# Grouping part-array attention matmuls in the planned order, and three pairs of heads with decay rows from SBUF

## The chip, the cores and the metric

The kernel runs on one core of one Trainium2 chip. The metric is the device time of one execution in microseconds; several executions of a kernel are timed and their median is given.

## The reference

A causal attention with a decay is followed by two feed-forward layers. The attention has 4 batches, 8 heads, 576 positions and 64 elements per head; each layer maps 2304 tokens of 512 elements to 2048 and back. All is float32.

```python
scores = scale * np.matmul(q, k.transpose(0, 1, 3, 2))
cum = np.cumsum(np.maximum(s, 0.0), axis=-1)
bias = -(cum[:, :, :, None] - cum[:, :, None, :])
scores = np.where(causal, -1e9, scores + np.minimum(bias, 0.0))
attn = softmax(scores)                      # along the last axis
x = attn @ v                                # then (tokens, 512)
h = x @ w_in                                # first layer
x = (h * np.clip(h + 3.0, 0.0, 6.0) / 6.0) @ w_out
h = x @ w2_in                               # second layer
out = (h * np.tanh(softplus(h))) @ w2_out
```

## The kernel before

**Stages.** Up to some 413 us the attention and the first layer for the first 1280 tokens run interleaved: the first layer's two matmuls for a slice of 128 of the 2048 inner elements (lines 889 and 929; each product is made of three rounded parts) stand between pieces of attention. Then come the first layer's remaining tokens (lines 1047 and 929) and the second layer in three blocks of columns (lines 1136 and 1220). In these later stages TensorE's matmuls follow each other in one fixed chain.

**Attention.** Heads are taken in pairs, one head on partitions 0 to 63 and one on 64 to 127. The first 256 positions of a batch are done by `small` (sixteen pairs), the rest by `unit` (sixteen pairs). In `small`, the scores of a pair are eight records of matmul (L772; four instructions, each profiled as two passes); each head uses half the rows of the array, so these are part-array matmuls. VectorE adds the decay and takes the maximum (L785), ScalarE takes the exponential (L792), VectorE or ScalarE scale (L812, L810), TensorE transposes (L818, whole array), the copy goes to `v`'s slot, and the product with V (L832) uses half the columns for each head, again part of the array. In `unit` the same steps are L637 (scores; the last tile of 288 columns uses the whole array), L644, L652, L683 (transposes) and L706 (product with V). The result of the first 256 positions goes into `blk`, the operand of the first layer, which can start when two batches' pairs have written the first part of it.

**Decay rows.** The cumulated sums of all heads are made on VectorE in one SBUF tile (`setup_b`), written to DRAM (`cums`), and loaded back for each pair, spread over 128 partitions, into a buffer `cb`; POOL sets the causal part in it (L758). The first pair alone (`fast`) doesn't load: TensorE adds the rows to the scores with a product of a column of the identity and the SBUF tile (L775, 32 rows of the array), and the mask comes from a constant.

**Weights.** They come as 64-bit words, 512 KB for a slice, into `wraw`, and are rebuilt to float32 by a step on ScalarE (L410) and several on VectorE (L420, L437, L451). The sixteen slices of w_in stay in sixteen slots `win`.

**Order.** Nothing in the order is written by hand. `Plan` takes nodes (an engine, a cost, a priority, the buffers they take and free) and makes a list schedule with them: at each moment the node of least priority that is ready, whose engine is free and whose buffers can be had, is put next on its engine. Buffers of a tag have a fixed number of slots (`MAP`). Where TensorE is planned to be idle in the first 70 us, filler matmuls on the identity are put (L352, one for each 0.11 us, at most 24). The instructions stand on each engine in the planned order, and each engine keeps to it. All priorities are worked out from the numbers in `T`. Loads and stores all go through SP's queue, in its order.

Of the kernel before, what the change touches and what calls it, by code (L numbers as in the profile page):

```python
# [10 lines left out]
F32 = mybir.dt.float32  # L11
# [6 lines left out]
NB, NH, S, D = 4, 8, 576, 64  # L18
DM, DFF = 512, 2048
P = 128  # L20
# [20 lines left out]
    "qk": ("att", 2, 7680), "cb": ("att", 2, 9472), "v": ("att", 2, 2560), "pt": ("att", 2, 10240), "nm": ("att", 2, 48),  # L41
    "l": ("att", 2, 48), "qkr": ("att", 1, 3840),
# [9 lines left out]
    xs=2.866, ls=11.367, sm=1.176, sm2=5.378, w0=4.591, w1=9.811, cum=11.658, wo=1.492, blk0=36.145, blk1=12.97,  # L52
    wo2=40.684, wo2r=9.728, win2=7.325, g=23.399, upre=9.483, uhalf=3.818, upost=6.415, uv=-2.503, spre=6.601,
    shalf=-1.839, spost=3.029, pe=5.342, bias=1.691, la=4, la2=2, wp=16.525, p0=-5.836, p1=6.148, p2=6.056, p3=56.106,
    xo0=7.372, lead=9.764, olead=6.509, c0=217.532, cs0=10.808, c1=61.463, cs1=11.269, gap=1.998, slead=4.439,
    p4=77.005, p5=96.709, s0=15.843, s1=21.887, s2=22.005, s3=14.562, s4=46.208, s5=30.366, xo1=5.675, lead1=6.3,
    olead1=5.945, wo3=2.932, gap1=-2.615, ks=0.781,
)
HOP = 0.05
# [23 lines left out]
class Node:  # L83
    __slots__ = ("eng", "cost", "fn", "deps", "prio", "new", "uses", "left", "succ", "ready", "end", "lat", "seq", "slack", "on", "idle", "start", "grant", "one", "bk", "bf", "tried")


class Plan:
# [8 lines left out]
    def add(self, eng, cost, fn, deps=(), prio=0.0, new=(), uses=(), lat=0.0):  # L96
# [9 lines left out]
        n.slack = 0.0  # L106
        n.grant = None
# [49 lines left out]
    def run(self):  # L157
# [22 lines left out]
        ring = 0.0  # L180
        left = len(self.nodes)
        pool.sort(key=lambda n: (n.prio, n.seq))
        while left:
            progress = True
            while progress:
# [3 lines left out]
                for n in pool:  # L189
# [12 lines left out]
                    if not self.can(n):  # L202
                        n.tried = self.ver
                        continue
                    self.take(n)
# [67 lines left out]
def mm_cost(n):  # L273
    return max(0.111, 0.01 + 0.000424 * n)
# [27 lines left out]
def tile_attention_moe_moe(ctx, tc, qk1, qk, v1, s, w_in, w_out, w2_in, w2_out, out):  # L302
# [273 lines left out]
    def unit(b, h, prio, step, dep0, depc, banks):  # L576
# [52 lines left out]
        for i, a, e in ((2, 0, 384), (3, 0, 512), (4, 0, 288), (4, 288, 576)):  # L629
# [9 lines left out]
            prev_s = A("PE", 3 * mm_cost(w) + (0.1 if i == 4 else 0.4), mm, [n_h, n_l, n_m, prev_s], prio, ps if prev_s else [*ps, nm, l], [t])  # L639
# [68 lines left out]
        n_pv = A("PE", 0.25 + 0.00178 * sum(nq - max(0, P * c - q0) for c in range(tb)), pv, n_p + [n_v], post, [po], [pt, vt])  # L708
# [25 lines left out]
    def small(b, h, pair, prio, step, dep0, depc, banks, fi, n_c1, n_id):  # L734
# [4 lines left out]
        raw = Buf("v", [P, 2 * N], F32)  # L739
# [678 lines left out]
```

## Time and profile before

| what | us |
|---|---|
| median of three runs | 947.76 (947.56 to 950.21) |
| the profiled execution | 945.56 |
| its span, first to last instruction | 943.7 |
| TensorE busy | 923.1 (98%) |
| VectorE busy | 721.3 (76%) |
| ScalarE busy | 599.3 (64%) |
| DMA engines, mean share | 71.4% |

The busy time of TensorE counts fillers as well, and a matmul's record lasts longer than its step in a row of matmuls, since they are pipelined. The step from one start to the next is therefore what a matmul costs in a row.

### The profile page before, as it was taken

To read this page: it belongs to the slowest core of one execution; us is meant where nothing else is said; L and a number is where in the kernel's file an instruction comes from. 1 tells how busy PE (TensorE), PEld (TensorE's weight loads), DVE (VectorE), ACT (ScalarE), POOL (GpSimd) and SP (SyncE) were. 2 spreads that over 40 slices of the span, in tenths; PEclk is the share of its full clock that TensorE was granted. 3 is DMA by queue.
4 is the path that set the end of the run, shared out by engine and by line. 5 is a ranking of instruction groups with operands and counts; after the bars stand their busy time and mean duration, and the time that the engine had idled before them with its cause. 6 is when DMAs were issued, how large, how long until landed. Compare 5 with 4: busy or idle time off the path is not lost.

```text
span 943.7 us, 16638 instructions
## 1 busy us (share of the span) xinstructions
PE 923.1 (98%) x5279; PEld 793.5 (84%) x5279; DVE 721.3 (76%) x1750; ACT 599.3 (64%) x1358; POOL 42.8 (5%) x102
## 2 busy tenths in 40 slices
PE   8999999999999999999999999999999999999998
PEld 5666677767777777988888888899999999999998
DVE  6998787977787555379869983987977779677774
ACT  5986776767665566457667544877556765566553
POOL 1111001111000101000000000000000000000000
PEclk8999999999999999999999999999999999999999
DMA  8798977899887876360029996769874498744785
GB/s 284 230 274 291 310 235 246 284 366 366 306 286 255 239 239 192 123 210 24 1 90 323 373 341 222 234 184 313 255 256 125 127 302 256 247 125 124 248 257 185
DMA packets 115350, 220.43 MB, mean 234 GB/s; under 512 B 12896, under 2 KB 51840, under 8 KB 115264
## 3 DMA queue, kind: packets, MB, share of 16 engines
q1 hardware_dynamic: 115264, 219.38, 71.4%
q8 instruction: 42, 0.69, 0.3%
q14 instruction: 44, 0.36, 0.1%
HBM read 176.76 MB, written 42.57 MB: 232 GB/s over the span
## 4 chain that ended last, share of the span: by engine, by line
PE 79%; DMA 10%; DVE 5%; ACT 3%; issue 1%; SPq 0%; POOL 0%; DVEq 0%; ACTq 0%; POOLq 0%
PE b L1220 18%; PE b L929 18%; PE b L1136 17%; PE b L1047 8%; PE b L889 7%; DMA wraw<-in_w_in_dram 4%; PE b L637 3%; PE b L706 3%; PE b L683 3%; DMA cb<-cuml 2%; DMA wraw<-in_w_out_dram 1%; DMA ws<-wtmp 1%; PE b L772 1%; PE b L352 1%; DMA wo<-wos 1%
## 5 line engine op out<-in xcount | busy, mean ns | idle before, releaser
L929 PE MATMUL b<-g,wo 128*128 128x512 f32 (+1 forms) x960 | 225.3, 376 | 0.2 <-DMA wo<-wos 0.2
L929 PEld LDWEIGHTS b<-g,wo 128*128 128x128 f32 x960 | 165.1, 189 | 33.4 <-issue 5.9
L889 PE MATMUL b<-blk,win 128*128 128x512 f32 (+1 forms) x576 | 137.6, 366 | 0.5 <-ACT blk L357 0.5
L1136 PE MATMUL b<-xob 128*128 128x384 f32 x648 | 117.8, 336 | 2.5 <-ACT b L357 1.8
L1136 PEld LDWEIGHTS b<-xob 128*128 128x128 f32 x648 | 112.3, 188 | 5.2 <-ACT b L357 2.7
L889 PEld LDWEIGHTS b<-blk,win 128*128 128x128 f32 x576 | 94.6, 189 | 19.0 <-issue 4.6
L652 ACT ACTIVATE cb<-cb,nm 128x384 f32<-128x384 f32 (+2 forms) x80 | 54.5, 682 | 27.7 <-DVE nm L644 26.3
L1136 PE MATMUL b<-xob,st 128*128 128x384 f32 x360 | 66.4, 336 | 0.9 <-ACT ub L357 0.4
L1136 PEld LDWEIGHTS b<-xob,st 128*128 128x128 f32 x360 | 62.4, 188 | 2.5 <-DVE e L1021 1.1
L458 DVE TENSOR_TENSOR xob<-xob 128x256 fp32r<-128x256 f32 x108 | 45.0, 422 | 22.5 <-ACT xob L357 20.1
L644 DVE CUSTOM_DVE_ANT_0 cb<-b,cb 128x384 f32<-128x384 f32 (+2 forms) x80 | 44.1, 586 | 21.2 <-PE b L637 17.4
L410 ACT ACTIVATE wtmp<-wraw 128x512 f32<-128x512 f32 x58 | 38.4, 666 | 29.4 <-DMA wraw<-in_w_in_dram 13.0
L357 ACT ACTIVATE b<-b 128x384 f32<-128x384 f32 (+1 forms) x64 | 32.1, 502 | 35.4 <-PE b L1136 22.6
L904 DVE TENSOR_TENSOR g<-e,g 128x512 fp32r<-128x512 f32 (+1 forms) x48 | 29.7, 619 | 31.7 <-ACT g L357 31.1
L1220 PE MATMUL b<-wo,xob 128*128 128x384 f32 x276 | 53.1, 334 | 0.0
L357 ACT ACTIVATE g<-win 128x384 fp32r<-128x384 f32 (+1 forms) x54 | 30.3, 568 | 33.3 <-PE b L929 21.5
L357 ACT ACTIVATE xob<-xob 128x256 fp32r<-128x256 f32 (+1 forms) x86 | 39.0, 457 | 17.1 <-DMA xob<-ws 15.7
L357 ACT ACTIVATE pt<-b 128x384 f32<-128x384 f32 (+2 forms) x89 | 42.5, 511 | 9.4 <-PE b L683 9.0
L1220 PEld LDWEIGHTS b<-wo,xob 128*128 128x128 f32 x276 | 48.3, 188 | 0.0
L637 PE MATMUL b<-qk 64*128 64x384 f32 (+2 forms) x288 | 44.7, 366 | 2.5 <-DVE nm L644 1.0
L1047 PE MATMUL b<-xob,wo 128*128 128x512 f32 x192 | 45.8, 392 | 0.3
L437 DVE SCALAR_TENSOR_TENSOR wtmp<-wraw,wtmp 128x512 uint32<-128x512 uint32 x64 | 44.3, 694 | 1.0
(201 smaller groups left out, 1761.2 us busy)
## 6 DMA issues: line engine op xcount, KB each, us to landing
xob<-ws SPq DMA_DIRECT2D x108, 256.0 KB, 3.5
wo<-wos SPq DMA_DIRECT2D x48, 512.0 KB, 5.4
wraw<-in_w_in_dram SPq DMA_DIRECT2D x32, 512.0 KB, 6.1
wraw<-in_w_out_dram SPq DMA_DIRECT2D x32, 512.0 KB, 5.6
st<-ws SPq DMA_DIRECT2D x60, 256.0 KB, 3.3
cb<-cuml SPq DMA_DIRECT2D x16, 896.0 KB, 7.9
xob<-ws SPq DMA_DIRECT2D x108, 128.0 KB, 2.2
ws<-xob SPq DMA_DIRECT2D x52, 256.0 KB, 5.7
```

Source lines behind the costliest of these rows:

```text
L357: nc.scalar.activation(out=out_, in_=in_, func=AF.Copy)
L410: nc.scalar.activation(out=tmp.t, in_=hi, func=AF.Prelu, scale=2.0 ** -112, alpha=-(2.0 ** 32))
L437: nc.vector.scalar_tensor_tensor(out=out_, in0=lo, scalar=29, in1=tu, op0=ALU.logical_shift_right, op1=ALU.bitwise_or)
L458: return a, add("DVE", v1x(n), lambda: nc.vector.tensor_tensor(out=l(), in0=r(l()), in1=r(h()), op=ALU.subtract), [a], prio, (), [buf])
L637: nc.tensor.matmul(out=ps[g].t[:, 0:w], lhsT=t.t[s_, ka, qo:qo + P], rhs=t.t[s_, kb, nk0 + a:nk0 + e], start=k == 0, stop=k == 2)
L644: nc.vector.tensor_tensor_reduce(out=p.t[:, o:o + w], in0=pb.t[:, 0:w], in1=cb.t[:, o:o + w], scale=-0.125, scalar=(3.0e38 if a == 0 else ...
L652: nc.scalar.activation(out=p.t[:, o:o + w], in_=p.t[:, o:o + w], func=AF.Exp, scale=-1.0, bias=nm.t[:, k:k + 1], accum_out=l.t[:, k:k + 1],)
L889: nc.tensor.matmul(out=hps.t[:, 0:N], lhsT=w.t[:, a, P * c:P * (c + 1)], rhs=x.t[:, c, b, 0:N], start=(c == 0 and k == 0), stop=(c == NCC ...
L929: nc.tensor.matmul(out=y[j].t[:, co[j]:co[j] + N], lhsT=wt.t[:, a, P * j:P * (j + 1)], rhs=g.t[:, b, 0:N], start=(f == 0 and k == 0 and no ...
L1047: nc.tensor.matmul(out=bank.t[:, 0:N], lhsT=lhs(a, j), rhs=xo[p].t[:, j, c, :], start=start and j == 0 and k == 0, stop=j == 1 and k == 2, ...
L1136: nc.tensor.matmul(out=bank.t[:, 0:NS], lhsT=w.t[:, a, P * j:P * (j + 1)], rhs=xo[p].t[:, j, b, :], start=start and j == 0 and k == 0, sto ...
L1220: nc.tensor.matmul(out=banks[m].t[:, 0:NS], lhsT=w.t[:, a, P * m:P * (m + 1)], rhs=b.t[:, c, :], start=start and f == 0 and k == 0, stop=f ...
```

## The change

- A node gets a `mode`: 1 for scores that use half the rows, 2 for products with V that use half the columns, 0 else. When TensorE is in a mode and the next node is of another one, the planner takes a ready node of the same mode instead if its priority is within `mw` = 6.281. Out of mode 0 a part-array node is held back for up to `hold` = 2.844 us when no other part-array node is ready and an ordinary one is. The planner's cost of a change of mode is 0.1 us into a mode and 0.207 back; the costs of the nodes themselves lose that part.
- Three pairs are `fast` instead of one. All pairs of the first two batches take their buffers from other tags: q and k in `st` (four slots) for `v`, the decay rows or scores in `win` for `cb` or `g`, V and the transposed rows in `win` for `qk`. The tiles of maxima and sums have four slots instead of two.
- The planner reckons 0.1 us instead of 0.05 for a hop between engines and 1.2 instead of 0.907 for a load's end, and 24 of the numbers in `T` have new values.

```diff
@@ T, the planner's numbers (two of the lines)
-    olead1=5.945, wo3=2.932, gap1=-2.615, ks=0.781,
+    olead1=5.945, wo3=2.932, gap1=-2.615, ks=0.703, mw=6.281, hold=2.844,
 )
-HOP = 0.05
+HOP = 0.1
@@ Plan.run
+                    if mode and n.one == "PE" and n.mode != mode:
+                        m = next((m for m in pool if m.one == "PE" and m.mode and m.ready <= t and m.prio <= n.prio + T["mw"] and m not in went and self.can(m)), None)
+                        if m is not None:
+                            n, best = m, ("PE", m.cost[0], 0.0)
+                    elif not mode and n.mode and now < n.ready + T["hold"] and not any(m.one == "PE" and m.mode and m is not n and m.ready <= t and self.can(m) for m in pool):
+                        m = next((m for m in pool if m.one == "PE" and not m.mode and m.ready <= t and m not in went and self.can(m)), None)
+                        if m is not None:
+                            n, best = m, ("PE", m.cost[0], 0.0)
                     self.take(n)
...
-                    if e == "PE" and now < 20.0:
-                        c *= 1.6
+                    if e == "PE":
+                        if now < 20.0:
+                            c *= 1.6
+                        if n.mode != mode:
+                            c += 0.1 if n.mode else 0.207
+                            mode = n.mode
...
-                        n.end = ring + 0.907
+                        n.end = ring + 1.2
@@ small
-        raw = Buf("v", [P, 2 * N], F32)
-        if fi and pair_no[0] % 2 == 0:
-            cb = Buf("g", [P, 2, 384], F32)
-        else:
-            cb = Buf("cb", [P, 2, 384], F32)
+        raw = Buf("st" if fi else "v", [P, 2 * N], F32)
+        cb = Buf("win" if fi else "cb", [P, 2, 384], F32)
...
-        v = Buf("qk", [P, 4 * D + 768], F32)
+        v = Buf("win" if fi else "qk", [P, 4 * D + 768], F32)
...
-        fast = fi and pair_no[0] <= 1
+        fast = fi and pair_no[0] <= 3
...
-        n_s = A("PE", 2.8 if fast else 0.9, mm, [n_ld, n_m, n_id], prio, pss + [nm, l] + ([cb] if fast else []), [raw] + ([setup_b] if fast else []))
+        n_s = A("PE", (2.8 if pair_no[0] <= 1 else 2.1) if fast else 0.76, mm, [n_ld, n_m, n_id], prio, pss + [nm, l] + ([cb] if fast else []), [raw] + ([setup_b] if fast else []))
+        n_s.mode = 1
```

What the planner makes of it is shown at three places. Line numbers of after stand 13 to 15 higher. First, TensorE behind the first pair of heads. Before, the first pair's scores and decay products (L772, L775) are followed by fillers on the identity:

```order
L772 MATMUL b_174<-v 128x256
L775 MATMUL b_174<-pt,ident 128x256
L772 MATMUL b_175<-v 128x256
L775 MATMUL b_175<-pt,ident 128x256
L352 LDWEIGHTS ident
L352 MATMUL b_254<-ident 128x256
L352 LDWEIGHTS ident
L352 MATMUL b_254<-ident 128x256
```

Now they are followed by the second and the third pair's (L785 and L788 are the same two lines); here is the end of the third, with the transposes (L832) and the products with V (L846) behind it:

```order
L785 MATMUL b_266<-st 128x256
L788 MATMUL b_266<-pt,ident 128x256
L785 MATMUL b_267<-st 128x256
L788 MATMUL b_267<-pt,ident 128x256
L832 MATMUL b_310<-ident,win 128x128 x3
L832 MATMUL b_321<-ident,win 128x128 x3
L832 MATMUL b_332<-ident,win 128x128 x3
L832 MATMUL b_339<-ident,win 128x128 x3
L846 MATMUL b_352<-win 64x256 x2
L846 MATMUL b_352<-win 64x128 x2
L846 MATMUL b_367<-win 64x256 x2
L846 MATMUL b_367<-win 64x128 x2
```

The 24 fillers are gone from there, and the first pair's transposes stand behind three pairs' scores instead of one.

Second, SP's queue in the first microseconds, with what each load waits for (DMAHW is an earlier load's landing). Before, from the third load of w_in on:

```order
L441 DMA wraw_220<-in_w_in_dram 128x512 [waits DMAHW2_49,DMAHW4_49,DVE_49,Activation_49]
L746 DMA v_224<-in_qk1_dram 128x512 [waits DMAHW3_49,PE_49]
L749 DMA cb_229<-cums_69 128x768 [waits DMAHW0_49]
L749 DMA g_233<-cums_69 128x768 [waits DMAHW5_49]
L749 DMA cb_238<-cums_69 128x768 [waits DMAHW6_49]
L441 DMA wraw_242<-in_w_in_dram 128x512 [waits DMAHW7_49,DVE_49,Activation_49]
L441 DMA wraw_297<-in_w_in_dram 128x512 [waits DMAHW2_49,DVE_49,Activation_49]
```

Now, from the sixth pair's load of q and k on to the load behind the fourth of w_in:

```order
L759 DMA st_284<-in_qk1_dram 128x512 [waits DMAHW6_49,PE_49]
L765 DMA win_290<-in_v1_dram 128x2x128 [waits DMAHW7_49]
L762 DMA win_294<-cums_69 128x768 [waits DMAHW0_49]
L765 DMA win_299<-in_v1_dram 128x2x128 [waits DMAHW1_49]
L762 DMA win_302<-cums_69 128x768 [waits DMAHW2_49]
L765 DMA win_307<-in_v1_dram 128x2x128 [waits DMAHW3_49]
L762 DMA win_314<-cums_69 128x768 [waits DMAHW4_49]
L759 DMA st_319<-in_qk1_dram 128x512 [waits DMAHW5_49,PE_49]
L455 DMA wraw_329<-in_w_in_dram 128x512 [waits DMAHW6_49,DVE_49,Activation_49]
L759 DMA st_411<-in_qk1_dram 128x512 [waits DMAHW7_49,PE_49]
```

The fourth load of w_in has moved behind two loads of q and k that wait for TensorE to have used the slot of an earlier pair.

Third, TensorE in the middle, around a product with V (L706 before, L721 now) of a `unit` pair. Before, it stands alone between transposes or scores and the first layer's matmuls:

```order
L637 MATMUL b_2787<-qk 128x288 x3
L637 MATMUL b_2793<-qk 128x288 x3
L889 MATMUL b_2766<-blk,win 128x512 x3
L706 MATMUL b_2803<-pt,v 64x320 x6
L706 MATMUL b_2803<-pt,v 64x192 x2
L706 MATMUL b_2803<-pt,v 64x64 x2
L929 MATMUL b_2822<-g,wo 128x512 x3
```

Now two pairs' products stand together:

```order
L944 MATMUL b_2549<-g,wo 128x512 x3
L721 MATMUL b_2775<-pt,v 64x320 x6
L721 MATMUL b_2775<-pt,v 64x192 x2
L721 MATMUL b_2775<-pt,v 64x64 x2
L721 MATMUL b_2792<-pt,v 64x320 x6
L721 MATMUL b_2792<-pt,v 64x192 x2
L721 MATMUL b_2792<-pt,v 64x64 x2
L944 MATMUL b_2563<-g,wo 128x512 x3
```

Over the whole program the blocks of part-array matmuls are 66 instead of 74, the fillers 83 instead of 113, and the instructions of every other kind on TensorE as many as before but for eight more decay products.

## Rows read from the trace of the kernel before

**Rows 1.** The page, busy time (us), share and instructions of each engine:

```profile
PE 923.1 (98%) x5279; PEld 793.5 (84%) x5279; DVE 721.3 (76%) x1750; ACT 599.3 (64%) x1358; POOL 42.8 (5%) x102
```

**Rows 2.** Stretches: length, then busy us of PE, PEld, DVE, ACT, POOL; clock; DMA share; GB/s:

```profile
26.40:54.00 27.60, 25.42 (x198) 17.79 (x195) 25.22 (x95) 24.43 (x83) 5.42 (x10) 1.00 0.83 255
54.00:70.00 16.00, 15.97 (x92) 11.22 (x90) 14.63 (x46) 14.55 (x39) 1.24 (x3) 1.00 0.91 263
70.00:413.00 343.00, 335.37 (x2077) 259.34 (x2074) 239.05 (x616) 218.85 (x502) 31.77 (x74) 1.00 0.81 268
```

**Rows 3.** Stretches of the start, for the granted clock (third number from the end):

```profile
5.70:9.00 3.30, 3.30 (x17) 2.00 (x15) 2.26 (x5) 0.66 (x1) 0.00 (x0) 1.00 0.88 274
9.20:11.40 2.20, 2.20 (x4) 0.87 (x4) 1.51 (x4) 1.18 (x2) 0.00 (x0) 0.50 0.83 291
12.40:15.80 3.40, 3.40 (x17) 2.34 (x18) 3.13 (x11) 3.27 (x13) 0.00 (x0) 0.50 0.90 264
```

**Rows 4.** Timeline of TensorE, 0 to 72 us: start, length (us), instruction, count:

```profile
6.18 0.48 PE L772 MATMUL b<-v 64*128 64x128 f32 x2
6.59 0.48 PE L775 MATMUL b<-pt,ident 32*128 32x128 f32 x2
...
7.83 0.70 PE L772 MATMUL b<-v 64*128 64x256 f32 x2
...
9.08 1.22 PE L772 MATMUL b<-v 64*128 64x256 f32 x2
10.23 1.22 PE L775 MATMUL b<-pt,ident 32*128 32x256 f32 x2
12.36 4.51 PE L352 MATMUL b<-ident 128*128 128x256 bf16 x24 [0.91 <-DVE nm L785]
16.71 0.82 PE L818 MATMUL b<-ident,g 128*128 128x128 f32 x6
...
18.30 1.58 PE L772 MATMUL b<-v 64*128 64x128 f32 x16
...
37.83 1.38 PE L352 MATMUL b<-ident 128*128 128x256 bf16 x11
39.04 0.83 PE L818 MATMUL b<-ident,cb 128*128 128x128 f32 x6
...
53.35 0.82 PE L818 MATMUL b<-ident,cb 128*128 128x128 f32 x6
```

**Rows 5.** Chain that ended last, 0 to 72 us: start, length without the overlap:

```profile
35.80 0.86 PE b L772 x8
...
37.09 0.80 PE b L832 x8
...
39.20 0.66 PE b L818 x6
```

**Rows 6.** Timeline of TensorE around one part-array block of the middle:

```profile
124.64 0.39 PE L929 MATMUL b<-g,wo 128*128 128x512 f32 x1
124.96 0.93 PE L772 MATMUL b<-v 64*128 64x128 f32 x8
125.81 2.35 PE L889 MATMUL b<-blk,win 128*128 128x512 f32 x9
128.00 0.82 PE L683 MATMUL b<-ident,cb 128*128 128x128 f32 x6
```

**Rows 7.** Chain that ended last, whole span: a long run of like matmuls:

```profile
496.62 87.07 PE b L929 x384
```

**Rows 8.** Timeline of POOL, 0 to 60 us: the first mask on loaded decay rows:

```profile
17.28 0.77 POOL L758 TENSOR_SCALAR_AFFINE_SELECT cb<-cb 128x256 f32<-128x256 f32 x2 [15.35 <-DMA cb<-cums]
```

**Rows 9.** Waits of TensorE, 70 to 413 us: total us, times, longest:

```profile
PE b L706 <- DMA v<-in_v_dram: 2.1, 1, 2.1
PE b L683 <- ACT cb L672: 1.3, 1, 1.3
```

**Rows 10.** Timeline of SP's queue, 0 to 72 us: fourth and fifth load of w_in:

```profile
12.68 3.87 SPq L441 DMA_DIRECT2D wraw<-in_w_in_dram  x2
```

More of the change, by code (lines that the diff above doesn't have):

```diff
@@ L40 @@
     "g": ("main", 2, 4096), "e0": ("main", 2, 2048), "st": ("main", 4, 2048), "wo": ("main", 3, 4096), "G1": ("main", 1, 3072),
-    "qk": ("att", 2, 7680), "cb": ("att", 2, 9472), "v": ("att", 2, 2560), "pt": ("att", 2, 10240), "nm": ("att", 2, 48),
-    "l": ("att", 2, 48), "qkr": ("att", 1, 3840),
+    "qk": ("att", 2, 7680), "cb": ("att", 2, 9472), "v": ("att", 2, 2560), "pt": ("att", 2, 10240), "nm": ("att", 4, 48),
+    "l": ("att", 4, 48), "qkr": ("att", 1, 3840),
     "xob": ("late", 1, 57344), "ub": ("late", 1, 6144),
@@ L83 @@
 class Node:
-    __slots__ = ("eng", "cost", "fn", "deps", "prio", "new", "uses", "left", "succ", "ready", "end", "lat", "seq", "slack", "on", "idle", "start", "grant", "one", "bk", "bf", "tried")
+    __slots__ = ("eng", "cost", "fn", "deps", "prio", "new", "uses", "left", "succ", "ready", "end", "lat", "seq", "slack", "on", "idle", "start", "grant", "one", "bk", "bf", "tried", "mode")
 class Plan:
@@ L106, in add @@
         n.slack = 0.0
+        n.mode = 0
         n.grant = None
@@ L180, in run @@
         ring = 0.0
+        mode = 0
         left = len(self.nodes)
@@ L638, in mm @@
                                          start=k == 0, stop=k == 2)
-            prev_s = A("PE", 3 * mm_cost(w) + (0.1 if i == 4 else 0.4), mm, [n_h, n_l, n_m, prev_s], prio, ps if prev_s else [*ps, nm, l], [t])
+            prev_s = A("PE", 3 * mm_cost(w) + (0.0 if i == 4 else 0.12), mm, [n_h, n_l, n_m, prev_s], prio, ps if prev_s else [*ps, nm, l], [t])
+            prev_s.mode = 0 if i == 4 else 1
             for g in range(len(ps)):
@@ L707, in pv @@
                                      start=c == 0, stop=c == tb - 1)
-        n_pv = A("PE", 0.25 + 0.00178 * sum(nq - max(0, P * c - q0) for c in range(tb)), pv, n_p + [n_v], post, [po], [pt, vt])
+        n_pv = A("PE", -0.06 + 0.00178 * sum(nq - max(0, P * c - q0) for c in range(tb)), pv, n_p + [n_v], post, [po], [pt, vt])
+        n_pv.mode = 2
         t0 = token(b, q0)
@@ L833, in pv @@
                                          rhs=v.t[:, 4 * D + 384 * g + 2 * a:4 * D + 384 * g + 2 * a + N - a], start=c == 0 and lhs is None, stop=c == 1)
-        n_pv = A("PE", 1.95 if fz else 0.9, pv, n_p + [n_v], post, [po, pn] if fz else [po], [v])
+        n_pv = A("PE", 1.75 if fz else 0.7, pv, n_p + [n_v], post, [po, pn] if fz else [po], [v])
+        n_pv.mode = 2
         pt_nodes.append(n_pv)
@@ L842, in small @@
         if fz:
-            held = Buf("st", [P, 512], F32)
+            held = Buf("e0", [P, 512], F32)
             src = lambda: held.t[:, 0:N]
```

12 lines of the change are left out of this document (6 added, 6 removed).

## Prediction

> **What bounds the kernel now.** I read the page first: TensorE is busy for 98% of the span [rows 1]. So time is won or lost where TensorE idles, runs filler matmuls, runs at the low clock, or is slowed between two kinds of work. The table of stretches shows where that is [rows 2]. From 70 to 413 us, in which attention and the first feed-forward layer are interleaved, TensorE is idle 7.6 of 343 us. Before 54 us things stand otherwise: from 26.4 to 54, VectorE and ScalarE are busy 25.2 and 24.4 of 27.6 us, and TensorE's share holds many fillers (L352): 89 of the program's 113 stand behind the first pair of heads. From 54 us on TensorE has hardly a gap. The start-up is thus a stretch with three near-full engines, and every microsecond that it gains or loses is passed on to the end, since nothing behind 54 us can absorb it.
>
> In the start the timeline of TensorE and the granted clock belong together [rows 3, 4]. The first pair A takes its decay rows from SBUF: each score product (L772, 64 rows) is followed by a decay product (L775, 32 rows) into the same bank. The clock granted is 1.00 (2.4 GHz) from 5.7 to 9 us and 0.50 (1.2 GHz) from 9.2 to 11.4 us, although TensorE has run without a pause; it comes back only after 3.5 us of full-array fillers, at some 15.9 us. The second pair's scores start at 18.30, since POOL had its decay rows only at 17.28 [rows 4, 8].
>
> **The change, part by part. (1) Two more pairs, B and C, take decay rows from SBUF.** Removed: two broadcast loads of 384 KB, two POOL masks, the wait to 17.28 and the 24 fillers from 12.36 to 16.7. Added: eight score products more slowly run and eight decay products. Prices: at the high clock 0.41 us for each 128-column product (6.18 to 6.59) and 0.63 for each of 256 columns (two from 7.83 to 9.08), so a pair is 4 x 0.41 + 4 x 0.63 = 4.15 us. At the low clock 256 columns take 1.15 (9.08 to 10.23) [rows 4]. 128 columns were not seen there; the difference of 0.22 between the two sizes doubles with a halved clock, which gives 0.72, and a pair 7.5 us. A pair with loaded rows is 0.86 [rows 5]. So the two pairs add 6.6 us of TensorE time at the high clock and 13.3 at the low one. I take the low one: the order has nothing but such products from A to the end of C, and it is these under which the clock fell. A ends at 11.45 as before, B at 18.95, C at 26.45.
>
> A page of the Trainium skill speaks of this too: "TensorE: Matmul & The Clock Gate", in its part on packing small matmuls, says that matmuls in distinct row groups run concurrently. By it the products of a pair's second head (rows 64 to 127) would run beside decay products (rows 0 to 31), and a pair would be a quarter shorter, the sum some 2 us less at the high clock. The row disagrees: products of 128 columns follow one another at 0.41 us whichever head they belong to [rows 4].
>
> From 26.45 I add up what the new order has on TensorE until the ninth pair's transposes are done, which before was 53.35 + 0.66 = 54.0 [rows 4, 5]: 9 transposes of 0.66, 8 products with V (L832) of 0.80, 7 scores of 0.86, 9 matmuls of the first layer at 0.227 [rows 7] and 52 fillers at 0.11 (eleven from 37.83 to 39.04): 5.9 + 6.4 + 6.0 + 2.0 + 5.7 = 26.0 us. Before, the same list from 16.7 on (with 8 scores, 21 first-layer matmuls and 65 fillers) makes 31.2 us and took 37.3, so 6.1 were waits and switches. I take 3.5 for after, since VectorE and ScalarE have been waiting for B and C and stand ready: 55.95. At that point 12 first-layer matmuls are still to do that had been done (2.7), one score is done that had not (0.86), and 7 fillers come later (0.8): 1.95 + 2.7 - 0.9 + 0.8 = **4.6 us lost** (4.55); with waits between 2 and 6.1, 3.1 to 7.2; at the high clock 2.1 gained. VectorE now waits for B's scores before it scales A's rows, which costs nothing, since A's transposes stand behind C's scores on TensorE in any case.
>
> **(2) First pairs in unused weight slots** (tags win and st for cb, g, qk, v) cost no instruction. They let loads go out early, but st has four slots: the fifth pair's load of q and k waits for A's scores, the sixth for B's, the seventh for C's, and SP is one queue. Behind the seventh stands the fourth load of w_in, so at 26.5 instead of 12.7 to 16.5 us [rows 10]. On SP and POOL the broadcasts and masks of two later pairs (tag cb) also stand ahead of the fourth pair's, whose scores are not due before some 30 us, 12 us after A to C's loads are through. I cost all this at nothing, since TensorE needs that weight only after some 56 us; without this cover it is the second rival below.
>
> **(3) Grouping.** The order has 66 blocks of part-array matmuls for 74. Behind the ninth pair 58 entries into a mode become 52, and 57 exits to the full array 48. A block's price is read at 124.64 us: the block starts 0.32 us after a second-layer matmul that is followed by the next at 0.227 (87.07 us for 384) [rows 6, 7]. From there to 128.00 are 3.36 us: one matmul and nine of the first layer make 2.27, so the eight score products cost 1.09. Eight that follow eight of their own kind add only 1.58 - 0.93 = 0.65 [rows 4, 6]. So a lone block costs 0.44 too much, about half of it at each end: 6 x 0.2 + 9 x 0.2 = **3.0 us gained**; bounds 1.9 (an entry at 0.32 - 0.227 = 0.09, an exit at the 0.15 by which the nine matmuls behind the block took longer) and 4.0 (nine whole blocks at 0.44).
>
> **(4) New priorities and latencies** in the planner (a hop 0.1 for 0.05 us, an SP load 1.2 for 0.907) reorder all engines. That no row shows. Of the 7.6 idle us from 70 to 413 the largest are single waits, 2.1 us for a V load and 1.3 us for a scaling on ScalarE [rows 2, 9]; a plan that reckons with later landings should meet fewer. Bounds: all of it gone, or 3 more. I take **2.0 gained**. Behind 413 us each matmul chain keeps its order: nothing.
>
> The sum is 4.6 - 3.0 - 2.0 = -0.4 us. The profiled execution took 945.56 (its span 943.7, 1.9 around it), which makes 945.2; the median of the runs shown, 947.76, stands 2.2 above it, so **947.4 us**. Its own range is about 942.5 to 952. A measurement of this kernel can tell about 0.3%, 2.8 us, from no change.
>
> **The rivals.** First: the clock is back, or stays, during B and C. For it: TensorE never pauses there, and at the low clock products of 256 columns fill it more evenly. Against it: the fall at 9.1 us in the midst of the same products [rows 3]. Then C ends 6.7 us earlier (13.3 - 6.6): 940.7. The Trainium skill's page "TensorE: Matmul & The Clock Gate", part on the clock gate, is on this side: it ties the high clock to a busy TensorE and the low one to an idle one. This case's rows speak against it, as the clock fell with no idle time before it.
>
> Second, slower: the held SP queue. With the seventh pair's load of q and k waiting for C's scores, weight loads four and five go out 10 us late or more, and those behind them with them. The DMA engines are 83% busy from 26.4 to 54, 91% to 70 and 81% to 413 [rows 2]. Some four loads of 512 KB, at 263 GB/s 2.0 us each, are 8 us of transfer that has to be fitted in again; if only 3 us of it find room before their readers come, TensorE waits 5: 952.4. It decides if TensorE idles for weights (blk,win or g,wo products) between 56 and 120 us.
>
> Third: the new order removes nearly all idle time of the middle, 7 us in place of 2, with the pairs at the low clock: 942.4. For it is that the big waits are few and single; against it, that a fixed order makes new ones where durations differ from the plan's, and the plan is 9 us out as soon as C ends (it gives the three pairs 11.2 us, the rows above 20).
>
> That the change would not group at all is excluded by the order itself.
>
> **How the numbers follow.** Forecast 0.41, high clock 0.26, held queue 0.22, middle emptied 0.11. Faster by over 0.3%: nearly all of the high clock and of the emptied middle, 0.36; slower: the held queue, 0.22; the rest, 0.42. The range goes from 940 (high clock, 940.7, with a little room) to 953 (held queue), which leaves out the farther halves of those two, under 0.2.
>
> **What will show it.** The third pair's last decay product ends at 26.5 us with the clock at 0.50 from 9 us on (low), or near 20 (high). The ninth pair's transposes end near 56 us. The fourth w_in load goes out right behind the third pair's scores. TensorE's idle time from 70 to 413 is 5 to 6 us, and its part-array blocks cost no more each than now. I am wrong on step 1 if C ends before 23 us, on step 2 if weights are waited for, on step 4 if the idle time of the middle rises.

## The result, and the profile after

| what | before | after |
|---|---|---|
| median, us | 947.76 (946.94 to 950.21, 7 runs) | 941.09 (936.26 to 942.68, 7 runs) |
| ratio of the medians | | 0.9918, 95% interval 0.9900 to 0.9936 |
| the profiled execution, us | 945.56 | 939.11 |
| its span, us | 943.7 | 937.3 |

The changed kernel is 0.8% faster, more than the 0.3% that can be told from no change. The forecast of little change, 947.4, was wrong; the time lies inside the range. By the number alone it is nearest to the first rival (940.7), but that is chance: what the trace shows is the third (942.4), as the clock stayed low under the three pairs and the middle lost its idle time. The page of after, the busy time of the engines:

```profile
PE 926.8 (99%) x5265; PEld 798.0 (85%) x5265; DVE 717.0 (76%) x1740; ACT 594.4 (63%) x1368; POOL 40.8 (4%) x98
```

The busy time of TensorE is larger than before [rows 1] in a shorter span, since slower products count as busy. The stretches show more (columns as in [rows 2]):

```profile
26.40:57.00 30.60, 29.56 (x234) 20.81 (x235) 24.57 (x113) 26.65 (x95) 2.60 (x6) 0.93 0.37 126
...
70.00:413.00 343.00, 341.06 (x2134) 267.32 (x2133) 250.81 (x647) 228.09 (x520) 30.88 (x72) 1.00 0.84 278
...
577.00:937.00 360.00, 354.77 (x2028) 351.11 (x2027) 272.48 (x606) 222.91 (x514) 0.00 (x0) 1.00 0.70 220
```

From 70 to 413 us TensorE's idle time is 343 - 341.06 = 1.9 us, where it was 7.6 [rows 2]. Its waits from 57 to 406 us (total us, times, longest) are three, and neither of those in [rows 9] is among them:

```profile
PE b L651 <- DVE nm L659: 1.1, 1, 1.1
PE b L698 <- ACT pt L371: 0.4, 1, 0.4
PE b L904 <- DVE e L916: 0.2, 1, 0.2
```

The DMA engines' share behind 26.4 us fell from 0.83 to 0.37. The start, first by its clock (stretches again), then on TensorE's timeline:

```profile
6.74:10.10 3.36, 3.36 (x14) 1.96 (x14) 1.08 (x3) 0.09 (x1) 0.00 (x0) 1.00 0.98 354
10.20:30.60 20.40, 20.40 (x57) 12.03 (x58) 10.07 (x41) 10.03 (x34) 5.29 (x12) 0.50 0.88 297
30.70:34.00 3.30, 2.92 (x28) 1.98 (x25) 2.50 (x12) 0.81 (x3) 0.00 (x0) 1.00 0.00 0
```

```profile
11.33 0.79 PE L785 MATMUL b<-st 64*128 64x128 f32 x2
12.05 0.79 PE L788 MATMUL b<-pt,ident 32*128 32x128 f32 x2
...
25.11 1.22 PE L788 MATMUL b<-pt,ident 32*128 32x256 f32 x2
26.26 2.82 PE L832 MATMUL b<-ident,win 128*128 128x128 f32 x12
...
56.35 0.94 PE L832 MATMUL b<-ident,cb 128*128 128x128 f32 x6
57.12 3.98 PE L904 MATMUL b<-blk,win 128*128 128x512 f32 x15
```

The third pair ends at 26.26 us, at the low clock from 10.2 us on. Two landmarks behind it, on the same timeline: the first matmul of the first layer's rest (L1047, after L1062) and of the second layer (L1136, after L1151), of before and then of after:

```profile
416.19 1.55 PE L1047 MATMUL b<-xob,win 128*128 128x512 f32 x6
...
583.53 1.22 PE L1136 MATMUL b<-xob 128*128 128x384 f32 x6
```

```profile
412.47 1.54 PE L1062 MATMUL b<-xob,win 128*128 128x512 f32 x6
...
579.55 1.22 PE L1151 MATMUL b<-xob 128*128 128x384 f32 x6
```

So after is 3.0 us late at the ninth pair's transposes (56.35 + 0.66 = 57.0, against 54.0), 3.7 early at the first layer's rest, 4.0 early at the second layer, and 6.4 early at the end. The gain was made in the interleaved middle, and some 2.4 us more in the second layer.

### The profile page after: what moved, and what is told of

The parts are those of the page before. It is cut to its first block, busy times and chain, and to the rows that moved or that the text cites. A ratio compares the mean times of both kernels' runs of the same rounds, so it can differ in the third digit from the quotient of the medians.

```text
span 937.3 us, 16531 instructions
## 1 busy us (share of the span) xinstructions
PE 926.8 (99%) x5265; PEld 798.0 (85%) x5265; DVE 717.0 (76%) x1740; ACT 594.4 (63%) x1368; POOL 40.8 (4%) x98
## 4 chain that ended last, share of the span: by engine, by line
PE 90%; DVE 4%; DMA 3%; ACT 2%; issue 1%; SPq 0%; POOL 0%; DVEq 0%; POOLq 0%; ACTq 0%
PE b L944 20%; PE b L1235 19%; PE b L1151 18%; PE b L904 10%; PE b L1062 8%; PE b L651 4%; PE b L721 3%; PE b L698 3%; PE b L785 2%; DMA wraw<-in_w_in_dram 1%; DMA wraw<-in_w_out_dram 1%; PE b L788 1%; PE b L366 1%; PE b L832 1%; PE b L846 1%
## 5 line engine op out<-in xcount | busy, mean ns | idle before, releaser
L944 PE MATMUL b<-g,wo 128*128 128x512 f32 (+1 forms) x960 | 223.2, 375 | 0.0
L944 PEld LDWEIGHTS b<-g,wo 128*128 128x128 f32 x960 | 165.2, 189 | 31.4 <-issue 4.7
L904 PE MATMUL b<-blk,win 128*128 128x512 f32 (+1 forms) x576 | 134.0, 365 | 0.2 <-DVE e L916 0.2
L1151 PE MATMUL b<-xob 128*128 128x384 f32 x660 | 121.7, 336 | 1.4 <-ACT b L371 1.2
L1151 PEld LDWEIGHTS b<-xob 128*128 128x128 f32 x660 | 114.7, 188 | 3.5 <-ACT b L371 1.8
L1151 PE MATMUL b<-xob,st 128*128 128x384 f32 x348 | 66.0, 335 | 0.6 <-ACT b L371 0.6
L371 ACT ACTIVATE g<-win 128x384 fp32r<-128x384 f32 (+1 forms) x57 | 32.3, 571 | 47.4 <-PE b L944 32.2
L1151 PEld LDWEIGHTS b<-xob,st 128*128 128x128 f32 x348 | 60.6, 188 | 1.4 <-ACT b L371 0.9
L371 ACT ACTIVATE xob<-xob 128x256 fp32r<-128x256 f32 (+1 forms) x107 | 45.8, 432 | 15.7 <-DMA xob<-ws 8.0
L424 ACT ACTIVATE wtmp<-wraw 128x512 f32<-128x512 f32 x58 | 38.9, 670 | 25.9 <-DMA wraw<-in_w_in_dram 13.8
L651 PE MATMUL b<-qk 128*128 128x288 f32 (+2 forms) x288 | 45.0, 363 | 1.1 <-DVE nm L659 1.1
L1062 PE MATMUL b<-xob,wo 128*128 128x512 f32 x192 | 45.6, 390 | 0.6 <-DVE xob L1020 0.6
L371 ACT ACTIVATE pt<-b 128x384 f32<-128x384 f32 (+2 forms) x85 | 40.6, 512 | 8.3 <-PE b L698 8.0
```

Of the source, the lines that this page charges most:

```text
L371: nc.scalar.activation(out=out_, in_=in_, func=AF.Copy)
L424: nc.scalar.activation(out=tmp.t, in_=hi, func=AF.Prelu, scale=2.0 ** -112, alpha=-(2.0 ** 32))
L651: nc.tensor.matmul(out=ps[g].t[:, 0:w], lhsT=t.t[s_, ka, qo:qo + P], rhs=t.t[s_, kb, nk0 + a:nk0 + e], start=k == 0, stop=k == 2)
L904: nc.tensor.matmul(out=hps.t[:, 0:N], lhsT=w.t[:, a, P * c:P * (c + 1)], rhs=x.t[:, c, b, 0:N], start=(c == 0 and k == 0), stop=(c == NCC ...
L944: nc.tensor.matmul(out=y[j].t[:, co[j]:co[j] + N], lhsT=wt.t[:, a, P * j:P * (j + 1)], rhs=g.t[:, b, 0:N], start=(f == 0 and k == 0 and no ...
L1062: nc.tensor.matmul(out=bank.t[:, 0:N], lhsT=lhs(a, j), rhs=xo[p].t[:, j, c, :], start=start and j == 0 and k == 0, stop=j == 1 and k == 2, ...
```

## The experiments

Two kinds were run. Some undo a part and let the planner make its order anew; the others hold the order of the changed kernel, instruction for instruction, and alter what one step costs.

**One fast pair instead of three, planned anew.**

```diff
-        fast = fi and pair_no[0] <= 3
+        fast = fi and pair_no[0] <= 1
```

> After with one pair of heads taking its decay rows from SBUF instead of three; the other first pairs keep the weight slots as buffers, grouping and new numbers stay, and the planner orders anew. Theory (the start-up of after is 4.8 us behind that of before at the ninth pair's transposes, and is passed on to the end): about 936 us, the ninth pair's transposes near 53 us instead of 57. Rival (the slow start costs nothing in the end, since later engines would have waited anyway): 940 to 942, with the gain at 55 us given back by 400.

944.71 us (943.43 to 947.07; ratio to before 0.9972, 0.9959 to 0.9985). The ninth pair's transposes are done 2.8 us earlier than in after: the matmul behind them starts at 54.36 for 57.12 us. At the first matmul of the first layer's rest nothing of that is left. It starts at 409.78 us, 2.7 earlier than in after, but 24 of the products of L944 that after has done by then, 0.12 us each, are still to come, 2.9 us. So it was lost in the middle and, next, at the handover from the interleaved middle to the first layer's rest. Two stretches, then the waits of TensorE in the second (total us, times, longest):

```profile
70.00:406.00 336.00, 331.41 (x2046) 255.39 (x2047) 241.28 (x632) 217.46 (x493) 32.05 (x72) 1.00 0.82 270
406.00:440.00 34.00, 30.34 (x165) 25.31 (x165) 32.94 (x58) 22.02 (x43) 0.00 (x0) 1.00 0.32 114
```

```profile
PE b L1062 <- ACT wo L371: 2.3, 2, 1.8
PE b L1062 <- DVE wo L518: 1.4, 2, 0.8
```

TensorE idles 4.6 us from 70 to 406, where after idles 1.9 (336 - 334.06), and 3.7 us at the handover, where after idles 0.59. The next run, with three pairs, has the same wait at the handover; so it goes with the new order and not with the number of pairs, and this run doesn't price the pairs.

**No grouping, planned anew.** The two preferences of the planner are never taken; its reckoned cost of a change of mode stays.

```diff
-                    if mode and n.one == "PE" and n.mode != mode:
+                    if False:
...
-                    elif not mode and n.mode and now < n.ready + T["hold"] and ...
+                    elif False and not mode and n.mode and now < n.ready + T["hold"] and ...
```

> After without the planner's two preferences for part-array blocks (the cost of a change of mode stays in its reckoning, so do the new numbers and the three pairs); 75 entries and 69 exits instead of 66 and 59. Theory (grouping is worth the changes it saves, nine entries and ten exits at about 0.2 us each): 3 to 4 us slower than after, 944 to 945, TensorE's idle time from 70 to 406 still about 2 us. Rival (grouping is also what removed the waits of the middle): 948 or more, idle time back at 6 to 8 us.

951.08 us (946.79 to 954.79; 1.0032, 1.0016 to 1.0049). From 70 to 406 us TensorE idles only 2.6 us, but at the handover stands the same wait (L1062 for ScalarE, 2.3 us in two waits):

```profile
406.00:440.00 34.00, 31.39 (x181) 26.71 (x180) 31.38 (x54) 20.44 (x42) 0.00 (x0) 0.95 0.43 147
```

The mean clock of that stretch is 0.95. By its time the run is the rival's, but the idle time of the middle did not come back, though the rival expected it to. So this run doesn't price the grouping alone either.

**Old numbers and latencies, planned anew**: T's values, HOP 0.05 and 0.907 as before, the rest as in after.

```diff
-HOP = 0.1
+HOP = 0.05
...
-                        n.end = ring + 1.2
+                        n.end = ring + 0.907
```

> After with the 22 old numbers, the hop at 0.05 and a load's end at 0.907; three pairs and grouping stay (64 entries, 60 exits). Theory (the new numbers removed some 5.7 us of waits of TensorE from 70 to 406 and 2.4 in the second layer): 947 to 950, idle time of the middle back at 6 to 8 us. Rival (grouping did it): 940 to 943.

959.27 us (957.15 to 963.87; 1.0135, 1.0105 to 1.0165), worse than either theory had it: 9.1 us idle from 70 to 406.

**Before, with the new numbers and latencies.**

```diff
-HOP = 0.05
+HOP = 0.1
```

> Before with the new numbers and latencies alone; one pair with rows from SBUF, no grouping, old buffers. Theory (the numbers alone remove the waits, and no slow start is paid): 939 to 941. Rival (the numbers are fitted to the rest of the change and do nothing alone): 946 to 950.

949.02 us (946.75 to 954.34; 1.0024, 1.0002 to 1.0047). Without the rest the new numbers bring nothing.

**Neighbours of the order.** The runs planned anew raised the question of what any other order costs. Three kernels move nearly all numbers of the planner by up to 1% at random; two are neighbours of after, one of before.

```diff
-    xs=2.866, ls=10.945, sm=1.176, sm2=5.326, w0=4.591, w1=9.811, cum=11.527, wo=1.492, blk0=29.215, blk1=14.81,
+    xs=2.845, ls=11.021, sm=1.182, sm2=5.3, w0=4.591, w1=9.801, cum=11.562, wo=1.501, blk0=28.978, blk1=14.67,
```

> The changed kernel with all of the planner's numbers but the two of the grouping moved by up to 1% at random, so that nothing that the change does is undone and the order is merely another of its neighbours (66 entries into part-array modes and 62 exits, for 66 and 59; 117 fillers for 83). It asks how much of the gain hangs on this one fitted order. Theory (the gain is that this order, as executed, has few waits; a neighbour has them again): 945 to 951, with idle time of TensorE from 70 to 406 us back above 3 us or a wait of some us at the handover to the first layer's rest behind 406 us. Rival (the gain comes from what the edits do, and neighbours have it too): 940 to 943.

> The changed kernel nudged by another draw of up to 1% (69 entries into part-array modes, 64 exits, 94 fillers). The first draw gave 961.5, of which 6.8 us were one wait at 420 us for VectorE and 3.0 one at 70 us. Theory (a neighbour has a few single large waits, at other places each time): 946 to 962, with one or two waits of TensorE above 1.5 us between 60 and 430 us. Rival (the first draw was an unlucky one): 940 to 944.

> The kernel before with all of its planner's numbers moved by up to 1% at random, with the same draw as in the nudged changed kernel. It asks if before was as closely fitted. Theory (each kernel's numbers were fitted until its order had few waits, so a neighbour of either is slower by several us): 952 to 968. Rival (before was an ordinary order and the changed kernel a lucky one): 944 to 950, as often below before's median as above it.

They took 961.53 (957.1 to 963.53), 959.17 (955.62 to 961.91) and 955.98 us (953.56 to 958.56): 20.4 and 18.1 us above after, 8.5 above before. Waits of TensorE in the first:

```profile
PE b L944 <- DVE g L919: 6.8, 1, 6.8
PE b L366 <- DVE nm L659: 2.8, 1, 2.8
```

and in the second:

```profile
PE b L944 <- DVE g L919: 8.8, 1, 8.8
PE b L366 <- DVE nm L659: 3.1, 1, 3.1
```

Two large waits stand in each. They were expected at other places each time, but stand at the same ones: the larger ends at the handover, at 427.7 and 426.6 us, the smaller in the middle, at 73.2 and 74.8. A 1% change of numbers that undoes nothing costs as much as undoing the numbers wholly, and more than undoing the grouping. None of the runs planned anew can therefore be put down to its edit. Such a wait also has a tail; stretches of the first neighbour (the clock is the third number from the end):

```profile
420.00:424.00 4.00, 0.88 (x5) 0.49 (x3) 4.00 (x5) 3.61 (x5) 0.00 (x0) 0.99 0.76 228
424.00:428.00 4.00, 0.29 (x1) 0.29 (x2) 3.99 (x5) 0.25 (x1) 0.00 (x0) 0.50 0.13 48
428.00:432.00 4.00, 4.00 (x25) 4.00 (x25) 1.92 (x6) 0.95 (x3) 0.00 (x0) 0.66 0.00 0
```

After 6.8 us without work the clock is at 0.50 (1.2 GHz), and TensorE's first 4 us behind the wait run at 0.66 in the mean.

**The order held: the start without decay products of B and C.**

```diff
+        decay = fi and pair_no[0] <= 1
...
-                                     start=True, stop=not fast)
-                    if fast:
+                                     start=True, stop=not decay)
+                    if decay:
```

> The changed kernel in its own order, instruction for instruction, but the second and the third pair leave out their decay products, so the decay is missing for the first 256 positions of four heads. It asks whether time won in the first 26 us arrives at the end when the order is held. In the changed kernel the third pair ends at 26.3 us (each pair 7.5 us, clock 0.50), the ninth pair's transposes at 57.0, and the median was 941.1. Theory (the start-up costs what the sum said, and is passed on whole): the eight score products of a pair take 0.86 us, so the third pair ends by some 13 us, limited by its load; VectorE and ScalarE, which were starved to 26 us, then set the pace to 57, and the ninth pair's transposes end 6 to 10 us earlier; the end comes as much earlier, 931 to 935. Rival A (the order was fitted to the late start: loads that were early enough are now late): the ninth pair's transposes end earlier by as much, but at the first matmul of the first layer's rest (412.5 us in the changed kernel) only half of it is left, 936 to 939. Rival B (VectorE and the masks set the pace to 57 us in any case): 940 or more.

933.07 us (930.87 to 934.04), 8.0 below after. The third pair is done by 13.8 us, but then TensorE waits. Its timeline:

```profile
11.63 2.15 PE L786 MATMUL b<-st 64*128 64x128 f32 x8 [1.18 <-issue]
15.24 1.51 PE L833 MATMUL b<-ident,win 128*128 128x128 f32 x6 [1.46 <-ACT win L807]
17.58 1.54 PE L833 MATMUL b<-ident,win 128*128 128x128 f32 x6 [0.82 <-ACT win L825]
19.05 2.51 PE L847 MATMUL b<-win 128*64 128x256 f32 x16
```

The products with V start at 19.05 us, 10.0 earlier than in after (29.01), and the first layer's rest at 402.95, 9.5 earlier. Of the 10.0, 1.2 belong to the execution and not to the edit, as the first pair began at 5.37 for 6.60 us. Time won in the start passes nearly whole through the middle; rivals A and B fall. The span is 8.2 us shorter (929.1): 1.3 are lost in the second layer.

**The order held: scores first, then decay products (SSDD for SDSD).**

```diff
-                    if fast:
-                        nc.tensor.matmul(
+                for g in range(2 if fast else 0):
+                    nc.tensor.matmul(
```

> The changed kernel in its own order, but inside each of the three first pairs the score products of both heads stand first and their two decay products behind them, for either half of the columns: SSDD where it was SDSD. It asks whether it is the alternation of 64-row and 32-row products that makes a product cost 0.41 us at the high clock and 0.72 at the low one (two heads' scores in a row are some 0.11 us each elsewhere in the program), and that goes with the fall of the clock at 10.2 us. Theory (the alternation costs most of it): a pair falls from 7.5 to some 5 us, the third pair ends at 17 to 21 us, the end comes 2 to 5 us earlier, 936 to 939. Rival (the price lies in the 32-row products themselves, or in the clock, whatever the order): the third pair ends at 25 to 27 us and the time is 940 to 942.

932.50 us (931.34 to 933.35; ratio to before 0.9845, 0.9819 to 0.9871): better than the theory had it. TensorE's timeline, the first pair and the end of the third, then a stretch for the clock:

```profile
6.60 0.49 PE L785 MATMUL b<-st 64*128 64x128 f32 x4
7.02 0.71 PE L788 MATMUL b<-pt,ident 32*128 32x128 f32 x4
...
9.34 0.49 PE L785 MATMUL b<-st 64*128 64x128 f32 x4
...
18.89 2.82 PE L832 MATMUL b<-ident,win 128*128 128x128 f32 x12
```

```profile
10.20:22.00 11.80, 11.80 (x41) 7.75 (x42) 9.21 (x40) 7.98 (x30) 2.39 (x6) 0.50 1.03 369
```

At the high clock a pair takes 2.74 us (6.60 to 9.34) for 4.15, and the third ends at 18.89 us for 26.26. Both executions begin the first pair at 6.60 us, so these 7.4 us are the edit's; the span is 7.8 shorter (929.6). Two heads' 128-column scores take 0.42 us together (6.60 to 7.02), as much as a single product did in the alternation [rows 4]. The clock still falls to 0.50.

The Trainium skill's page "TensorE: Matmul & The Clock Gate", in its part on packing small matmuls, says that matmuls in distinct row groups run concurrently. The trace agrees for the two heads' scores, rows 0 to 63 and 64 to 127, when they stand together.

**The order held: decay products on all 128 rows.** The tile of sums is cleared once.

```diff
+        nc.vector.memset(setup_b.t[:, 0:384], 0.0)
...
-  lhsT=ident[0:NB * NH, row + g:row + g + 1].to_broadcast([NB * NH, P]),
-  rhs=rows()[3][:, COFF[i]:COFF[i] + CW[i]],
+  lhsT=ident[:, row + g:row + g + 1].to_broadcast([P, P]),
+  rhs=setup_b.t[:, COFF[i]:COFF[i] + CW[i]],
```

> The changed kernel in its own order, but the decay products of the three first pairs use all 128 rows of the array: the tile of sums is cleared once on all partitions, by one more VectorE step of 384 columns in the first microseconds, and the product takes the identity's whole column. It asks whether the clock falls at 10.2 us because these products leave most rows of the array unused. Theory: with 128 rows in half of the products the clock stays at 1.00 in 10.2 to 26 us, or comes back early, the third pair ends near 20 us as in the rival of the prediction, and the end comes 4 to 6 us earlier, 935 to 937. Rival (the clock falls in any case): third pair at 26 us, 940 to 942; if a change between 64 and 128 rows costs more than one between 64 and 32, up to 944.

932.47 us (930.43 to 933.73; ratio 0.9841, 0.9816 to 0.9867). The clock, and the end of the third pair on the timeline:

```profile
5.70:18.00 12.30, 12.30 (x49) 7.16 (x49) 10.02 (x39) 6.49 (x22) 0.00 (x0) 1.00 1.04 377
```

```profile
17.53 0.70 PE L789 MATMUL b<-pt,ident 128*128 128x256 f32 x2
18.06 1.62 PE L833 MATMUL b<-ident,win 128*128 128x128 f32 x12
```

The clock holds at 1.00 through the three pairs. That is no chance of this execution: the mean granted clock of the whole span is 1.000 in all six executions of this kernel, and 0.989 to 0.991 in the seven of after. Products in alternation cost 0.41 and 0.63 us as before, so the alternation's price is the same for 32 and 128 rows, and only the clock differs. The third pair ends 8.2 us earlier, 1.0 of it because the first began at 5.64 for 6.60 us, and the span is 8.7 shorter (928.6).

**Both together.** 

> The changed kernel in its own order with the two edits of before put together: inside the three first pairs both heads' scores and then both decay products, and decay products on all 128 rows. Each edit alone gave 932.5. At the high clock a pair in this order took 2.74 us (the first pair of that run, 6.60 to 9.34), so with the clock held three pairs end 8.2 us behind 5.64, at 13.9 us, where the pairs of either edit alone ended at 18 to 19. Theory (it was the time of the three pairs that cost, and the rest follows): the clock stays at 1.00 and the end comes up to 4 us earlier, 928.5 to 930. Rival (below 18 us VectorE and ScalarE set the pace, as in the run without decay products, whose scores were done at 13.8 and whose transposes still waited for ScalarE until 15.2 and 17.6): no more than 1.5 us earlier, 931 to 933, with idle time of TensorE behind the third pair and perhaps the low clock after it.

930.90 us (929.25 to 933.13; ratio 0.9817, 0.9791 to 0.9842), the fastest kernel here, though its interval overlaps those of either edit alone. TensorE's timeline, the second pair's end, the third's begin, and the second transposes, then a stretch for the clock:

```profile
9.98 1.13 PE L789 MATMUL b<-pt,ident 128*128 128x256 f32 x4
12.24 0.99 PE L786 MATMUL b<-st 64*128 64x128 f32 x4 [1.13 <-issue]
...
18.19 0.92 PE L833 MATMUL b<-ident,win 128*128 128x128 f32 x6 [0.53 <-ACT win L825]
```

```profile
11.10:18.00 6.90, 5.39 (x23) 3.72 (x22) 6.76 (x31) 5.63 (x21) 0.00 (x0) 0.75 1.05 373
```

The second pair ends 1.13 us before the third can start, and the products with V start at 19.05 as without decay products. The time lies between the theory and the rival; the timeline is the rival's: below some 18 us the pairs are no longer what bounds the start. The clock did not hold here: behind the wait of 1.13 us it fell to 0.50 at 14.6 us, in the third pair, for all that the decay products use 128 rows, and was back at 18.0.

**The order held: six blocks taken apart again**, on the kernel with full-row decay products. Where two blocks of one mode stand together behind 70 us, the second is moved behind the next whole-array node.

```diff
+            if b.start < 70.0 or not a.mode or a.mode != b.mode or c.mode:
+                continue
...
+            order.insert(j, order.pop(i))
```

> The kernel with full-row decay products (932.5 us) in its own order but for TensorE's in six places behind 70 us, where two blocks of the same part-array mode stand together: there the second block is moved behind the next whole-array node. So six more blocks are entered and left, which is about what the grouping of the change saved (66 entries for 74), and nothing else moves by more than that node's length. It prices the grouping with the order held, which no replanned kernel could. Theory (a lone block costs 0.44 us too much, as the prediction read it, with 0.24 as its lower bound): the stretch from the ninth pair's transposes (47.0 us) to the first matmul of the first layer's rest (403.4) grows by 1.4 to 2.6 us and the time is 934 to 935. Rival (much of a block's price is hidden, or lies elsewhere): the stretch grows by less than 0.8 us and the time is 932 to 933. If moving the six blocks makes new waits of TensorE, these are read from the trace and taken out.

934.63 us (933.8 to 937.52) for 932.47. Side by side with the kernel without the moves, TensorE's sequence is later from just before each move to the second matmul behind it, where the delay settles, by 0.35, 0.34, 0.34, 0.39, 0.39 and 0.33 us, 2.1 in all. So a block costs 0.36 us, and the stretch grows as the theory had it. The profiled execution, the slowest of the four, is some 4.8 us later still at the first layer's rest, which is not the moves' own price. Most of that, 3.5 us, comes in one place behind the third move, where scores now wait for VectorE. TensorE's timeline, and a stretch behind it for the clock:

```profile
176.26 2.33 PE L922 MATMUL b<-blk,win 128*128 128x512 f32 x9
179.99 1.44 PE L669 MATMUL b<-qk 64*128 64x512 f32 x6 [1.40 <-DVE nm L677]
```

```profile
180.00:184.00 4.00, 4.00 (x14) 2.77 (x15) 2.85 (x8) 2.89 (x9) 1.15 (x3) 0.72 0.94 325
```

The wait is 1.40 us; most of the rest comes with the clock, 0.72 in the 4 us behind it.

The Trainium skill's page "TensorEngine Tiling (Array Packing)" says under "Key Properties" that a change of tiling mode drains the engine. The trace agrees in so far as a change costs time, 0.36 us here for a way in and out; the drain itself it doesn't show.

**Old late numbers.** Five of the planner's numbers as before (`ls` stands in another line); TensorE's order differs from the second layer on alone.

```diff
-    xo0=7.036, lead=9.764, olead=8.187, ..., gap=0.466, slead=4.334,
+    xo0=7.372, lead=9.764, olead=6.509, ..., gap=1.998, slead=4.439,
```

> The changed kernel with five of the planner's numbers (ls, olead, xo0, gap, slead) put back to their values of before. The order is the same instruction for instruction up to the first matmuls of the second layer and differs behind that alone. It asks what of the gain is made in the second layer, which the prediction took to be none. Theory (these numbers removed the waits at the edges of its blocks): 943 to 944, with the 2.5 us that the changed kernel won between the second layer's first and last matmul gone (356.3 us from one to the other before, 353.8 in the changed kernel), and the time up to 579.5 us unchanged. Rival (that part was chance of the run): 940.5 to 941.5.

940.77 us (938.68 to 941.9): by the time, the rival. The trace says otherwise. From the first matmul of the second layer (577.23) to the first of the last six (932.05) are 354.8 us, in after (579.55 to 932.52) 353.0. Waits of TensorE in the second layer, of after and then of this kernel:

```profile
PE b L1151 <- ACT b L371: 1.8, 3, 0.6
PE b L1151 <- DVE ub L1036: 0.2, 1, 0.2
```

```profile
PE b L1151 <- ACT b L371: 2.1, 4, 0.6
PE b L1151 <- DVE st L472: 0.7, 1, 0.7
PE b L1151 <- DVE ub L1036: 0.3, 1, 0.3
```

In this execution the first pair began earlier (5.83 us for 6.60) and the clock fell later (third pair's end at 23.58 us for 26.26), which hid the 1.8 us. The times cannot settle it: the two ratios to before, 0.9917 and 0.9918, have intervals of 0.2% to either side, as much as is asked for. The five kernels that hold after's order can help, since they are the same in the second layer, instruction for instruction. They take 353.3 to 354.3 us for this stretch, this kernel 354.8 and before 355.5. So the new numbers do win time there, but after's 353.0 is the best of six: 1.2 to 2.5 us against before, of which these five numbers make 0.5 to 1.8.

## Why the prediction was wrong, step by step

**Step 1, pairs B and C: right.** A pair was to take 7.5 us at the low clock and took 7.46 (11.33 to 18.79); C was to end at 26.45 and ended at 26.26. The first rival (high clock) falls for this kernel: TensorE was busy for all of the 20.4 us that the clock was low. That the end was hit to 0.2 us is luck all the same, since the moment of the fall isn't fixed: 9.1 us before, 10.2 here, 11.8 in the run with old late numbers, whose third pair ends at 23.58. One part was too small: the clock stayed low for 4 us behind C, so twelve transposes took 2.75 us and the sixteen products with V behind them 2.3. The ninth pair's transposes ended at 57.0 for 55.95, which with the prediction's own account of work still to do makes 5.6 us lost for 4.6, inside its bounds. That this time passes on to the end was assumed there; the held orders showed it. One row was read too widely: products follow one another whichever head they belong to in the alternation alone. With nothing between them, two heads' scores run together, 0.42 us for both.

**Step 2, free slots and SP's queue: right.** The fourth w_in load went out at 25.65 us, beside C's last products. No matmul from 57 to 406 us waited for a weight; the longest wait there is 1.1 us, for VectorE. The second rival falls. The DMA share fits that: from 2 to 26.4 us it was 0.98, for 0.85 before, as the early pairs' loads had gone out, and behind it 0.37, so that the engines had room.

**Step 3, grouping: right, a little too large in price.** 3.0 us rested on 0.44 for a lone block. The six moves give 0.36. For the 6 entries and 9 exits fewer, 7.5 blocks, that is 2.7 us, inside the bounds of 1.9 to 4.0.

**Step 4, the new order: here it failed, in size.** The prediction took 2.0 us of 7.6 in the middle and wrote "Behind 413 us each matmul chain keeps its order: nothing". The idle time from 70 to 413 us fell by 5.7 us, and the second layer gained some 2.4 in this execution, 1.2 to 2.5 by all that hold its order. The single waits of [rows 9] are both gone. The third rival described this and was given 0.11, on the argument that a fixed order makes new waits where durations differ from the plan's. That argument is right of an arbitrary order: the neighbours have 7 to 9 us in one wait. It doesn't hold of this one, which has a single wait above 0.6 us from 57 to 413. Why this order escapes is not shown. Nothing in the trace of before could tell that, but the bounds could have warned: "all of it gone" stood 5.6 us away from the value taken, and for the second layer no row of its waits was looked at, though its order comes from the same planner. The sign named for an error here, a rise of the idle time, looked one way only.

The account closes to about 1 us: 5.6 lost in the start, 3.7 + 5.6 = 9.3 gained from there to the first layer's rest (5.7 of it idle time, some 2.7 changes of mode, 0.9 not resolved; the steps from one matmul's start to the next, idle time left out, are 3.8 us shorter there at equal numbers, so the 0.9 is no wait either), 0.3 to the second layer, and 2.4 in it: 6.4 us, as the spans say. The forecast's sum with 5.6, 2.7 and 5.7 in the places of its first three terms, and 2.4 for the second layer in place of nothing, gives 940.4 for the profiled execution, which took 939.11.

**What stays open.** How the 5.7 us of idle time divide among the grouping preference, the new numbers and the early loads can't be told: each undone alone gives a wholly different order, and neighbours of one order differ by 18 us and more. Which of the nudged numbers makes the wait of 7 to 9 us at 420 us wasn't tried.

## What to carry to other kernels

When an order comes from a planner with fitted numbers, undoing one part and planning anew measures the loss of the fit, not the part: hold the order and change what one step costs. Give the term "a new order" a range as wide as the idle time that the order could remove, and look for it in every stage that the planner touches. Where time is known to pass through, mend the dearest step in place: either of two edits of a few lines to the first three pairs won 8.6 us, more than the change's 6.7.

## What the runs showed of the hardware

- With TensorE busy throughout, the clock fell to 0.50 at 10.2 us under products of 64 and 32 rows in turn, and stayed at 1.00 when those of 32 rows used 128, all else in place, in each of six executions. Putting scores together did not keep it, and with both edits it fell at 14.6 us, behind a wait of 1.13 us.
- Products of alternating row groups cost 0.41 us each for 128 columns whether the second has 32 or 128 rows; two scores on rows 0 to 63 and 64 to 127 standing together cost 0.42 for both, two 32-row products behind them 0.63 (7.02 to 7.65).
- A wait can cost more than itself: behind 6.8 us without work the clock was 0.66 in the next 4 us, behind 1.4 us it was 0.72. It need not: in the 4 us behind before's wait of 2.1 us [rows 9] it was 1.00, and so it was in the whole middle of after.
- The start of the low clock varies from execution to execution (10.2 us in after, some 11.8 in the run with old late numbers). The third pair's end differs by 2.7 us between these two, 0.8 of it because the first pair began earlier.
